# Attention, a dense layer and a top-2 expert layer in one kernel: three quarters of expert 0's converted weights are kept between its two parts

## The chip, the cores and the metric

One core of a Trainium2 chip runs the whole computation as one program. The metric is the device time of one execution in microseconds (us). The engines are TensorE (PE, with its weight loads shown apart as PEld), ScalarE (ACT), VectorE (DVE), GpSimd (POOL) and SyncE (SP). In this kernel SP issues the plain transfers between HBM and SBUF, and POOL issues the gathers and scatters that take their rows from a list.

## The reference

Three layers follow one another. All inputs are float32.

```
attention: q, k, v of 2 x 8 heads x 576 x 64
  scores = q k^T / 8; only the 32 largest of a row stay; softmax; times v
  -> x of 1152 tokens x 512
dense layer: h = x w_in (512 x 2048); g = max(h,0) + alpha min(h,0); x = g w_out (2048 x 512)
expert layer: 8 experts, each w1[e] (512 x 1024) and w2[e] (1024 x 512)
  logits = x w_gate + softplus(x w_noise) * noise; the best two experts of a token, softmax weights p
  out[token] = sum over its two experts of p * ( max(x w1[e], 0) w2[e] )
```

## The kernel before

**Precision.** Every float32 product is made of three matmuls on split operands. A weight tile is converted into a high part (a rounded copy, written by ACT) and a low part (raw minus high, written by DVE). The products are high times high, high times low and low times high.

**Order of the work.** The order of instructions on each engine is written out by a planner (class `Order`, line 136). Pieces of the kernel are generators that ask for an engine with a cost and a rank. The planner plays this through with its own clock and, whenever an engine is free in that play, emits the waiting step of lowest rank. The chip then runs each engine's list in that order, and each instruction waits for what it needs. Named counts such as `take("w2i", room=3)` and `give("w2i")` stand for buffers. When PE has nothing to do in the play, the planner may emit filler matmuls on a tile of ones (line 1728). It does so until the first block of expert 0's late part (line 1841).

**The dense layer** goes through the tokens in five groups of tiles. The last group (tiles 7 and 8) ends near 530 us. Behind it the gate runs for that group (`gate`, line 1051). It ranks the experts (a matmul into `pt`, line 1093, with the operand `g_ohb`), writes the slot lists with four scatters (line 1131, POOL), and expert 0's `oh` is made from `g_rm` (lines 1097 and 1239). When all groups have their slots, SP reads the lists back as `meta` (line 1187), and POOL gathers the tokens' rows by them (line 1323).

**The expert layer.** Each expert has 336 slots for tokens. Its weights are handled in four quarters `ch`, 256 of the 1,024 hidden columns each. A quarter has two halves: `half` 0 is a part of w1 (tile `w2i`) and `half` 1 a part of w2 (tile `w2o`). `weights2(e, ch, half, late)` (line 1271) takes one of five `raw2` buffers, loads 512 KB into it (for w1 of experts 0 and 1 in four transfers of 128 KB, line 1282; for w2 one transfer, line 1278), takes one of three `w2i` or `w2o` buffers, and converts with one ACT (line 1298) and one DVE instruction (line 1301) on 128x1024. The `raw2` buffer comes free after the DVE instruction.

**Expert 0 has two parts** (NE = 1). Slots are handed out in the order of the groups, and the kernel counts on the first four groups to fill its first 128 slots (a flag at the end tests that). So an early part can run while the last group's gate is being worked out: `early_block(0, ch)` (line 1417) for ch 0 to 3 does 12 matmuls of w1 (line 1438), two transposes (line 1452) and six matmuls of w2 (line 1472), and frees its `w2i` and `w2o` buffers behind each quarter. Then `x_part(0, d)` (line 1393) builds the operand for the other 208 slots in four steps, partly from `oh` (matmul at line 1408, ACT at line 1410, DVE at line 1412). The late part, `expert_block(0, fb)` (line 1482) for fb 0 to 7, does these 208 slots in blocks of half a quarter (12 matmuls at line 1507, the rest at line 1549). It goes through the quarters in the order 0, 1, 2, 3, and all four are loaded and converted a second time for it. An early quarter's buffers come free behind its early block. So the second conversions of quarters 0, 1 and 2 stand among the early blocks and the x_part steps, and those of quarter 3 behind block fb 1.

**Expert 1** follows. Its rows are gathered by `meta` and turned by PE (`x_part(1, d)`, line 1404). Its first weights take the buffers that expert 0's late part frees. Experts 1 to 7 use 336 slots in full.

Of the kernel before, what the change touches and what calls it, by code (L numbers as in the profile page):

```python
# [55 lines left out]
NE = 1  # L56
# [79 lines left out]
class Order:  # L136
# [107 lines left out]
    def give(self, what):  # L244
        self.held[what] -= 1
        self.given[what] = self.now
        self.at(self.now, 1, self.scan)

    def mark(self, *what):
        self.made.add(what)  # L250
        self.at(self.now, 1, self.scan)
# [12 lines left out]
def block_kernel(ctx: ExitStack, tc: tile.TileContext, q, k, v, w_in, w_out, alpha,  # L264
# [19 lines left out]
    order = Order()  # L284
# [986 lines left out]
    def weights2(e, ch, half, late=True):  # L1271
        yield need("b1")
        yield take("raw2", room=NRW)
        b1 = room["b1"]
        yield DMA, 1.5, 2.0
        raw = b1.tile([128, 1024], F32, name="raw2", bufs=NRW)
        if half:
            nc.sync.dma_start(raw.rearrange("p (c d) -> p c d", c=2),
                              w2[e][ch * 256:(ch + 1) * 256, :].rearrange("(c p) d -> p c d", p=128))
        elif e < NX:  # L1280
            for b in range(4):
                nc.sync.dma_start(raw[32 * b:32 * b + 32].rearrange("p (q f) -> p q f", q=4),
                                  w1[e][128 * b:128 * b + 128, ch * 256:(ch + 1) * 256].rearrange("(q p) f -> p q f", q=4))
        else:
            nc.sync.dma_start(raw.rearrange("p (c f) -> p c f", c=4),
                              w1[e][:, ch * 256:(ch + 1) * 256].rearrange("(c p) f -> p c f", p=128))
        tag = ("w2i", "w2o")[half]
        yield take(tag, room=3)
        wt = b1.tile([128, 2, 1024], R32, name=tag, bufs=3)
        W2[e, ch, half, late] = wt  # L1290
        turned = half and late and YT[0] <= e < YT[1]
        yield ACT, 0.95 + 0.1 * turned
        his, los, raws = [wt[:, 0]], [wt[:, 1]], [raw]
        if turned:
            his, los = ([in_order(wt[:, i, 512 * c:512 * c + 512]) for c in range(2)] for i in range(2))
            raws = [in_turns(raw[:, 512 * c:512 * c + 512]) for c in range(2)]
        for hi, x in zip(his, raws):
            nc.scalar.activation(hi, x, AF.Copy)  # L1298
        yield DVE, dve(1024) + 0.1 * turned
        for hi, lo, x in zip(his, los, raws):  # L1300
            V.tensor_sub(lo, x, split(hi))  # L1301
        yield FIN
        give("raw2")
        mark("w2", e, ch, half, late)

    def gather_x(e):
        yield need("b1")
# [109 lines left out]
    def early_block(e, ch):  # L1417

        yield need("w2", e, ch, 0, False)
        yield need("xe0", e)  # L1420
        for t in range(len(GROUPS[-1])):
            yield need("y1", len(GROUPS) - 1, 15)
        if (e, ch) != (0, 0):
            yield need("h0", *((e, ch - 1) if ch else (e - 1, 3)))
        else:
            yield take("yo", room=2)
            HN[0] = room["b1"].tile([128, CJ, DM], F32, name="yo", bufs=2).rearrange("p j d -> p (j d)")
        wh, wl = (W2[e, ch, 0, False][:, i].rearrange("p (c f) -> p c f", c=4) for i in range(2))
        xh, xl = (x[:, :, 0:CP] for x in XE[e])
        bank = yield take("h_ps", "s_ps")  # L1430
        steps = [(l, d, r) for d in range(4) for l, r in ((xh, wh), (xh, wl), (xl, wh))]
        for n, (l, d, r) in enumerate(steps):
            if n % 4 == 0:
                yield PE, 4 * 0.109
            if n == 0:
                h_ps = ps.tile([128, 2, 512] if bank == "s_ps" else [128, 512], F32, name=bank)
                h_ps = h_ps[:, 0, 0:256] if bank == "s_ps" else h_ps[:, 0:256]
            nc.tensor.matmul(h_ps, l[:, d, :], r[:, d, :], start=(n == 0), stop=(n == 11))
        mark("h0", e, ch)
        yield FIN  # L1440
        give("w2i")
        yield ACT, actp(256), 0, -EB
        hn = HN[0][:, 256 * ch:256 * ch + 256]
        nc.scalar.activation(hn, h_ps, AF.Relu)
        yield FIN
        give(bank)
        yield take("hh", room=3)
        bank = yield take("pt", "x_ps")
        yield PE, 0.22
        pt = ps.tile([128, 4, 128], F32, name=bank)  # L1450
        for i in range(2):
            nc.tensor.transpose(pt[:, i, :], hn[:, 128 * i:128 * i + 128], ident)
        yield ACT, actp(256), 0, -EB
        hh, hl = (room["b1"].tile([128, w], R32, name=n, bufs=3)[:, 0:256].rearrange("p (c t) -> p c t", c=2)
                  for n, w in (("hh", WIDTH), ("hl", CAP)))
        nc.scalar.activation(hh, pt[:, 0:2, :], AF.Copy)
        yield DVE, dve(256), 0, -EB
        V.tensor_sub(hl, pt[:, 0:2, :], split(hh))
        yield FIN
        give(bank)  # L1460
        if ch:
            yield need("y0", e, ch - 1)
        else:
            if not e:
                yield take("y")
            Y0[e] = ps.tile([128, DM], F32, name="y%d" % e)
        yield need("w2", e, ch, 1, False)
        bh, bl = (W2[e, ch, 1, False][:, i].rearrange("p (c d) -> p c d", c=2) for i in range(2))
        for i in range(2):
            yield PE, 0.648  # L1470
            for n, (l, r) in enumerate(((hh, bh), (hh, bl), (hl, bh))):
                nc.tensor.matmul(Y0[e], l[:, i, :], r[:, i, :], start=(ch == 0 and i == 0 and n == 0),
                                 stop=(ch == 3 and i == 1 and n == 2))
        mark("y0", e, ch)
        yield FIN
        give("hh")
        give("w2o")
        if (e, ch) == (NE - 1, 3):
            give("yo")
        mark("y0d", e, ch)  # L1480

    def expert_block(e, fb):

        ch, s = divmod(fb, 2)
        turned = YT[0] <= e < YT[1]
        yield need("w2", e, ch, 0, True)
        js = range(int(e < NE), CJ)
# [298 lines left out]
    for g, ts in enumerate(GROUPS):  # L1786
        t = max(t, ready[g])
        late = g == len(GROUPS) - 1
# [15 lines left out]
    FB = 3.7  # L1804
# [17 lines left out]
    for e in range(E):  # L1822
        te = t + e * TE
        if e < NX:
            ranks["xe", e] = te - 12.0
            order.add(te - 12.0, x_parts(e))
        if e >= NH:
            order.add(te - (XR if e >= NX else XN), gather_x(e))
        for ch in range(4):
            for half in range(2):  # L1830
                order.add(te + (2 * ch - 4 + half) * FB, weights2(e, ch, half))
        for fb in range(8):
            order.add(te + fb * FB, expert_block(e, fb))
        if e:
            order.add(te + 4 * FB, gather_partner(e))
        ranks["out", e] = te + TE
        order.add(te + TE, expert_out(e))
# [221 lines left out]
```

## Time and profile before

| what | value |
|---|---|
| time, median of 3 runs | 817.0 us (814.26 to 824.21) |
| the profiled execution: time | 811.02 us |
| its span, first to last instruction | 809.3 us |
| PE busy | 752.3 us (93%) |
| DVE busy | 606.2 us (75%) |
| ACT busy | 506.4 us (63%) |
| POOL busy | 358.1 us (44%) |
| data moved | 156.62 MB, mean 194 GB/s |

The profile is of one execution. Times are counted from the start of its span. An engine's busy time contains no register, branch or semaphore work; busy PE contains the filler matmuls too. A row of a timeline gives in brackets how long the engine sat idle before that instruction, and whose end released it by the profile's inference. The granted clock is 1.00 where PE has its full 2.4 GHz, and 0.50 where it has 1.2 GHz.

### The profile page before, as it was taken

The page shows a single profiled execution, that of the slowest core. Times are in us where ns is not written, and L with a number is a line of the kernel's source. Part 1 is how long each engine was busy: PE and PEld are TensorE (multiplying, and loading weights), DVE is VectorE, ACT ScalarE, POOL GpSimd, SP SyncE. Part 2 cuts the span into 40 slices and gives each one's busy share as a digit, 9 for nine tenths or more (in the row PEclk, how much of TensorE's full clock was granted, in tenths as well). Part 3 has the DMA queues.
Part 4 walks back from the last instruction along what each step waited for, and adds up shares of the span by engine and source line. Part 5 has one row for each costly group of instructions (what it writes and reads, how often), then busy time and mean ns, then how long its engine had stood idle before and what let it go on. Part 6 is the DMA issues. An engine that isn't in the chain of part 4 may idle for free. (4 is left out here: it accounts for less than half of the span.)

```text
span 809.3 us, 15510 instructions
## 1 busy us (share of the span) xinstructions
PE 752.3 (93%) x5238; PEld 685.8 (85%) x5238; DVE 606.2 (75%) x1713; ACT 506.4 (63%) x1081; POOL 358.1 (44%) x402
## 2 busy tenths in 40 slices
PE   8999878769999999999999999989899998999994
PEld 6888767668898998899988988878799997999983
DVE  6999999998988888898889545167567756667632
ACT  6878897897588778576747642264545544455331
POOL 3655665665575555454445434302422424131313
PEclk9999998688999999999999999999999999999998
DMA  9444689851446402465247559988889988986631
GB/s 277 138 157 122 196 284 321 291 177 64 134 148 193 156 28 94 150 229 181 104 132 234 183 181 304 347 218 198 239 247 242 264 212 245 254 255 180 203 103 59
DMA packets 99851, 156.62 MB, mean 194 GB/s; under 512 B 15902, under 2 KB 65582, under 8 KB 99764
## 3 DMA queue, kind: packets, MB, share of 16 engines
q1 hardware_dynamic: 94260, 145.04, 58.6%
q0 software_dynamic: 5504, 10.51, 4.5%
q8 instruction: 43, 0.70, 0.4%
q14 instruction: 44, 0.36, 0.1%
HBM read 126.76 MB, written 29.34 MB: 193 GB/s over the span
## 5 line engine op out<-in xcount | busy, mean ns | idle before, releaser
L672 POOL TENSOR_TENSOR low<-s_sb,low 128x576 f32<-128x576 f32 x72 | 102.5, 1425 | 81.6 <-ACT low L670 81.6
L948 PE MATMUL h_ps<-xh,wi 128*128 128x256 f32 (+1 forms) x576 | 123.9, 294 | 3.3 <-DVE gf L966 2.6
L948 PEld LDWEIGHTS h_ps<-xh,wi 128*128 128x128 f32 x576 | 98.0, 196 | 8.4 <-DVE gf L966 4.4
L633 DVE MAX8 tk<-rest 128x8 f32<-128x296 f32 x216 | 97.7, 459 | 1.1
L992 PE MATMUL y<-wo,gh 128*128 128x512 f32 x288 | 96.7, 417 | 1.3 <-ACT gh L976 1.3
L979 POOL TENSOR_TENSOR gl<-gf,gh 128x256 fp32r<-128x256 f32 (+1 forms) x80 | 56.6, 709 | 67.3 <-ACT gh L976 65.5
L948 PE MATMUL h_ps<-xl,wi 128*128 128x256 f32 (+1 forms) x288 | 83.4, 289 | 0.0
L717 PE MATMUL x_ps<-vb,pT 128*128 128x64 f32 (+1 forms) x640 | 79.7, 270 | 3.7 <-ACT pT L696 3.3
L717 PEld LDWEIGHTS x_ps<-vb,pT 128*128 128x128 f32 (+1 forms) x640 | 74.7, 187 | 9.9 <-ACT pT L696 6.6
L1298 ACT ACTIVATE w2o<-raw 128x512 fp32r<-128x512 f32 (+1 forms) x60 | 40.4, 711 | 57.2 <-PE x_ps L1542 31.6
L1301 DVE TENSOR_TENSOR w2o<-raw,w2o 128x512 fp32r<-128x512 f32 (+1 forms) x60 | 45.5, 790 | 35.6 <-ACT w2o L1298 28.8
L1507 PE MATMUL s_ps<-xeh,w2i 128*128 128x336 f32 (+1 forms) x256 | 64.9, 315 | 3.8 <-DVE hl L1523 3.8
L1542 PE MATMUL y<-hh,w2o 128*128 128x336 f32 (+1 forms) x288 | 66.9, 316 | 0.0
L636 DVE MATCH_REPLACE8 rest<-tk,rest 128x296 f32<-128x296 f32 x144 | 64.8, 451 | 0.0
L1507 PE MATMUL h_ps<-xeh,w2i 128*128 128x336 f32 (+1 forms) x256 | 63.3, 313 | 0.4 <-DVE hl L1523 0.4
L676 ACT ACTIVATE low<-low,bias 128x576 f32<-128x576 f32 x72 | 55.7, 774 | 12.3 <-POOL low L672 12.2
L582 PE MATMUL s_ps<-kp,qt 128*128 128x288 f32 (+2 forms) x336 | 60.9, 310 | 1.9 <-DVE rest L616 1.9
L598 ACT ACTIVATE s_sb<-s_ps 128x576 f32<-128x576 f32 x72 | 46.9, 651 | 22.9 <-PE s_ps L582 22.3
L992 PE MATMUL y<-wo,gl 128*128 128x512 f32 x144 | 58.6, 407 | 2.1 <-POOL gl L979 1.4
L670 ACT ACTIVATE low<-s_sb,bias 128x576 f32<-128x576 f32 x72 | 55.6, 774 | 7.7 <-POOL bias L641 7.6
L1323 POOL DMA_INDIRECT xg<-x,meta x21 | 25.7, 1225 | 72.2 <-DMA xl<-xg 28.9
L948 PEld LDWEIGHTS h_ps<-xl,wi 128*128 128x128 f32 x288 | 56.5, 196 | 0.7 <-issue 0.3
(315 smaller groups left out, 2069.4 us busy)
## 6 DMA issues: line engine op xcount, KB each, us to landing
raw<-in_moe_w_dram SPq DMA_DIRECT2D x60, 512.0 KB
wi<-wsc SPq DMA_DIRECT2D x48, 512.0 KB
wo<-wsc SPq DMA_DIRECT2D x48, 512.0 KB
raw<-in_moe_w_in_dram SPq DMA_DIRECT2D x16, 512.0 KB
raw<-in_moe_w_out_dram SPq DMA_DIRECT2D x16, 512.0 KB
wsc<-wi SPq DMA_DIRECT2D x16, 512.0 KB
wsc<-wo SPq DMA_DIRECT2D x16, 512.0 KB
raw<-in_moe_w_dram SPq DMA_DIRECT2D x48, 128.0 KB
```

The lines of the kernel that those rows point to most:

```text
L582: nc.tensor.matmul(s_ps[:, j, o:o + c1 - c0], l, r[:, c0:c1], start=(i == 0), stop=(i == len(steps) - 1 and (c < 4 or c1 != S)))
L633: V.max(tk[:, 8 * i:8 * i + 8], src)
L636: V.match_replace(rest, tk[:, 8 * i:8 * i + 8], src, -3.0e38)
L670: nc.scalar.activation(low, SC[ht], AF.Relu, bias=bi[:, 1:2], scale=-BIG)
L672: nc.gpsimd.tensor_sub(low, SC[ht], low)
L676: nc.scalar.activation(low, low, AF.Exp, bias=bi[:, 0:1], scale=SCALE, accum_out=SM[part][:, col:col + 1])
L717: nc.tensor.matmul(o, pT[:, i, cs], vb[b, hh // 2][:, s, i * 64:(i + 1) * 64], start=(first and hh == h and i == 0), stop=False)
L948: nc.tensor.matmul(h_ps, l[:, d, :], r[:, d, 0:gn], start=(n == 0), stop=(n == 11))
L979: nc.gpsimd.tensor_sub(gl, gf, split(gh))
L992: nc.tensor.matmul(Y1[g][t], l[:, t * 128:(t + 1) * 128], r, start=(i == 0 and n == 0), stop=(i == 15 and n == 2))
L1507: nc.tensor.matmul(h_ps, l[:, d, s * 128:(s + 1) * 128], r[:, d, :], start=(n == 0), stop=(n == 11))
L1542: nc.tensor.matmul(YP[e][b][:, 0:c], l[:, s, bs], r[:, 0:c], start=(fb == 0 and n == 0), stop=(fb == 7 and n == 2))
```

## The change

In the early part the buffers of quarters 1, 2 and 3 are no longer given back. Their tiles are entered a second time under the late part's key, and the late part's need is marked as met with the early one. The late part takes the quarters in the order 3, 2, 1, 0. Only quarter 0 is loaded and converted again. Its request stands at the rank that quarter 3 had, and it takes the buffer that comes free when the late part has used quarter 3. Experts 1 to 7 are asked for as before.

```
--- before.py
+++ after.py
@@ -1302,6 +1302,9 @@
         yield FIN
         give("raw2")
         mark("w2", e, ch, half, late)
+        if not late and ch:
+            W2[e, ch, half, True] = wt
+            mark("w2", e, ch, half, True)
 
     def gather_x(e):
         yield need("b1")
@@ -1438,7 +1441,8 @@
             nc.tensor.matmul(h_ps, l[:, d, :], r[:, d, :], start=(n == 0), stop=(n == 11))
         mark("h0", e, ch)
         yield FIN
-        give("w2i")
+        if not ch:
+            give("w2i")
         yield ACT, actp(256), 0, -EB
         hn = HN[0][:, 256 * ch:256 * ch + 256]
         nc.scalar.activation(hn, h_ps, AF.Relu)
@@ -1474,7 +1478,8 @@
         mark("y0", e, ch)
         yield FIN
         give("hh")
-        give("w2o")
+        if not ch:
+            give("w2o")
         if (e, ch) == (NE - 1, 3):
             give("yo")
         mark("y0d", e, ch)
@@ -1482,6 +1487,8 @@
     def expert_block(e, fb):
 
         ch, s = divmod(fb, 2)
+        if e < NE:
+            ch = 3 - ch
         turned = YT[0] <= e < YT[1]
         yield need("w2", e, ch, 0, True)
         js = range(int(e < NE), CJ)
@@ -1828,7 +1835,10 @@
             order.add(te - (XR if e >= NX else XN), gather_x(e))
         for ch in range(4):
             for half in range(2):
-                order.add(te + (2 * ch - 4 + half) * FB, weights2(e, ch, half))
+                if e >= NE:
+                    order.add(te + (2 * ch - 4 + half) * FB, weights2(e, ch, half))
+                elif ch == 3:
+                    order.add(te + (2 * ch - 4 + half) * FB, weights2(e, 0, half))
         for fb in range(8):
             order.add(te + fb * FB, expert_block(e, fb))
         if e:
```

## Rows read from the trace of the kernel before

**Rows 1.** Page, part 1: busy us over the span, share, instructions.
```profile
PE 752.3 (93%) x5238; PEld 685.8 (85%) x5238; DVE 606.2 (75%) x1713; ACT 506.4 (63%) x1081; POOL 358.1 (44%) x402
```

**Rows 2.** Stretches: length, busy PE, PEld, DVE, ACT, POOL, clock, DMA share, GB/s.
```profile
548.00:556.00 8.00, 7.24 (x51) 6.13 (x50) 7.86 (x19) 3.62 (x7) 4.75 (x4) 1.00 0.61 172
...
556.00:562.00 6.00, 6.00 (x44) 5.22 (x41) 2.40 (x5) 1.71 (x4) 0.00 (x0) 1.00 1.11 262
...
690.00:768.00 78.00, 78.00 (x509) 78.00 (x509) 52.50 (x87) 38.26 (x69) 22.10 (x18) 1.00 0.75 224
```

**Rows 3.** The same view, line 1301 alone: length, DVE, clock, DMA share, GB/s.
```profile
548.00:556.00 8.00, 5.86 (x5) 1.00 0.61 172
```

**Rows 4.** Instructions of lines 1298 and 1301: ns min/median/max, first and last start.
```profile
L1298 ACT ACTIVATE w2i<-raw x36: 1041/1052/1062, 477.0 to 771.2; 128x1024 fp32r<-128x1024 f32 x36
...
L1301 DVE TENSOR_TENSOR w2i<-raw,w2i x36: 1179/1225/1226, 478.1 to 772.3; 128x1024 fp32r<-128x1024 f32 x36
```

**Rows 5.** Timeline, PE, 545 to 557: start, us, line, operation [idle before, releaser].
```profile
545.11 0.17 PE L1093 MATMUL pt<-g_ohb,upper 128*128 128x8 bf16 x1 [1.33 <-DVE hl L1458]
...
550.92 0.82 PE L1728 MATMUL y<-ones 128*128 128x256 bf16 x6
...
552.23 0.67 PE L1406 MATMUL pt<-ident,xg 128*128 128x128 f32 x4 [0.49 <-DVE xel L1412]
...
554.90 1.47 PE L1728 MATMUL y<-ones 128*128 128x256 bf16 x12
...
556.13 0.34 PE L1507 MATMUL h_ps<-xeh,w2i 128*128 128x208 f32 x1
```

**Rows 6.** Timeline, ACT, 541 to 545.
```profile
541.96 1.06 ACT L1298 ACTIVATE w2i<-raw 128x1024 fp32r<-128x1024 f32 x1 [2.67 <-DMA raw<-in_moe_w_dram]
...
543.28 1.04 ACT L1298 ACTIVATE w2o<-raw 128x1024 fp32r<-128x1024 f32 x1
...
544.23 0.37 ACT L1456 ACTIVATE hh<-pt 128x256 fp32r<-128x256 f32 x1
```

**Rows 7.** Timeline, DVE, 544 to 551; five conversions stand from 549.54 to 556.
```profile
544.98 1.22 DVE L1301 TENSOR_TENSOR w2o<-raw,w2o 128x1024 fp32r<-128x1024 f32 x1
...
546.11 0.17 DVE L1097 SCALAR_TENSOR_TENSOR g_rm<-pt,g_ohb 128x16 f32<-128x16 f32 x1
...
549.46 0.17 DVE L1127 TENSOR_SCALAR mi<-g_pos 128x4 int32<-128x4 f32 x1
...
549.54 1.22 DVE L1301 TENSOR_TENSOR w2o<-raw,w2o 128x1024 fp32r<-128x1024 f32 x1
```

**Rows 8.** Timeline, POOL, 549 to 567: the four scatters and the first gather.
```profile
549.91 1.77 POOL L1131 DMA_INDIRECT slots<-mi,si  x1 [21.34 <-DVE mi L1127]
...
551.99 1.01 POOL L1131 DMA_INDIRECT slots<-mi,si  x1 [0.30 <-issue]
...
554.58 0.99 POOL L1131 DMA_INDIRECT slots<-mi,si  x1 [0.30 <-issue]
...
565.77 1.05 POOL L1323 DMA_INDIRECT xg<-x,meta  x1 [10.20 <-issue]
```

**Rows 9.** Timeline, SP's queue: the read of the slots.
```profile
560.53 0.38 SPq L1187 DMA_DIRECT2D meta<-slots  x1
```

**Rows 10.** Chain that ended last: start, us, what; two transfers' landings.
```profile
568.46 6.28 DMA xg<-x,meta
...
773.18 3.65 DMA ysc<-yo
```

**Rows 11.** Timeline, PE, 573 to 575: transposes of expert 1's rows.
```profile
573.99 0.33 PE L1404 MATMUL pt<-ident,xg 128*128 128x128 f32 x1 [1.74 <-issue]
...
574.78 0.29 PE L1404 MATMUL pt<-ident,xg 80*128 80x80 f32 x1 [0.47 <-DMA xg<-x,meta]
```

**Rows 12.** Timeline, PE, at 681; then the stretch behind it, as rows 2.
```profile
681.75 0.42 PE L1507 MATMUL s_ps<-xeh,w2i 128*128 128x336 f32 x1 [3.78 <-DVE hl L1523]
...
681.70:685.20 3.50, 3.45 (x13) 3.46 (x14) 3.50 (x7) 2.48 (x6) 0.00 (x0) 0.57 0.60 186
```

More of the change, by code (lines that the diff above doesn't have):

```diff
@@ L1304, in weights2 @@
         mark("w2", e, ch, half, late)
+        if not late and ch:
+            W2[e, ch, half, True] = wt
+            mark("w2", e, ch, half, True)
     def gather_x(e):
@@ L1440, in early_block @@
         yield FIN
-        give("w2i")
+        if not ch:
+            give("w2i")
         yield ACT, actp(256), 0, -EB
@@ L1476, in early_block @@
         give("hh")
-        give("w2o")
+        if not ch:
+            give("w2o")
         if (e, ch) == (NE - 1, 3):
@@ L1484, in expert_block @@
         ch, s = divmod(fb, 2)
+        if e < NE:
+            ch = 3 - ch
         turned = YT[0] <= e < YT[1]
@@ L1830, in block_kernel @@
             for half in range(2):
-                order.add(te + (2 * ch - 4 + half) * FB, weights2(e, ch, half))
+                if e >= NE:
+                    order.add(te + (2 * ch - 4 + half) * FB, weights2(e, ch, half))
+                elif ch == 3:
+                    order.add(te + (2 * ch - 4 + half) * FB, weights2(e, 0, half))
         for fb in range(8):
```

## Prediction

> **What bounds the kernel now.** I read the page first, then the busy times by stretch, then the timelines of PE, ACT, DVE, POOL and SP around the change, and last the chain that ended last. The page shows PE busy for 752.3 of 809.3 us [rows 1]. The stretches say where that holds. From 690 to 768, in the middle of the expert layer, PE is busy for 78.00 of 78.00 us, and what is done on another engine there is hidden [rows 2]. From 548 to 556, between expert 0's early and late part, DVE is the full engine: 7.86 of 8.00 us, of which the conversions of line 1301 are 5.86 us in five instructions [rows 2, 3]. PE looks busy there too, but part of it is filler on `ones` [rows 5]. So a gain has to come out of the few places before expert 1 where PE waits or fills.
>
> I find four such places. The gate's matmul at 545.11 came after 1.33 us of idle time, released by DVE's `hl` [rows 5]. From 550.92 to 552.23 there are six fillers and a wait of 0.49 us for `xel`, together 1.31 us [rows 5]. From 554.90 to 556.13 there are twelve fillers before the late part's first matmul, 1.23 us [rows 5]. And the transposes of expert 1's rows wait 1.74 and 0.47 us for the gather [rows 11]. Beside PE runs a second path: the gate's last DVE step at 549.46, four scatters, SP's read of the slots at 560.53, POOL's gather from 565.77, its landing 6.28 us behind 568.46, at 574.74 [rows 7 to 10]. Both paths meet at the transposes, and there the gather is the later one.
>
> **What is removed.** Six of the eight second conversions go, with their loads. On ACT that is 6 x 1.05 = 6.3 us, on DVE 6 x 1.22 = 7.3 us [rows 4]. On SP it is 3 x 4 + 3 x 1 = 15 transfers of 6 x 512 KB = 3 MB. In time the places that empty are the early ones, those of quarters 0, 1 and 2. The pair that stays stands where quarter 3's pair stood, behind block fb 1. No matmul goes.
>
> **PE's own path.** The wait of 1.33 us: ACT's `hh` at 544.23, which feeds that `hl`, stood behind a second conversion (541.96, which had itself waited 2.67 us for its load) and an early one (543.28) [rows 6]. The first goes, so ACT can be 1.06 us or more ahead. The price lies between 0 and 1.33 us, and I take 1.33, since the queue loses 1.06 us of work and 2.67 us of waiting. The 1.31 us: the `xel` steps stand between conversions of 1.22 us on DVE, all five from 549.54 on are second ones, and all five go [rows 3, 7]. Between 0 and 1.31, I take 1.31. The 1.23 us of fillers cover the same queue ahead of the last `xel`, and go too. PE reaches the transposes 1.33 + 1.31 + 1.23 = 3.87 us earlier.
>
> **The gather's path.** The gate's chain on DVE starts with `g_rm` at 546.11, right behind a conversion of 544.98 that ends at 546.20 (starts and ends overlap by the pipeline) [rows 7]. Its matmul is at 545.11 [rows 5]. The matmul moves by 1.33 us. The wait behind the conversion, 546.11 - 545.11 = 1.00 us less the matmul, is gained as well if that early conversion moves ahead. So between 1.33 and 2.3 us; I take 1.8. The last scatter ends at 554.58 + 0.99 = 555.57, and SP can read at 560.53, so landing takes 4.96 us, and the read 5.24 us until the first gather at 565.77 [rows 8, 9]. Both lie in a stretch with a DMA share of 1.11 [rows 2], which is weight loads. With five `raw2` buffers, the loads that are next after the early part (expert 0's quarter 0, expert 1's quarter 0, half of its quarter 1) all fit at once, and are done before the scatters; the next one has to wait for a conversion behind fb 1. For an emptier path the nearest row is a store that landed in 3.65 us [rows 10]. So the landing gains 0 to 1.3 us and the read 0 to 1.6 us. I take 0.7 for each, the middle, since one row of another kind is not much. The first scatter took 1.77 us and a later one 1.01 us [rows 8]. That gives 0 to 0.8 us, and I take 0, since the later ones also ran beside conversions. The gather itself stays amid weight loads: 0. The sum is 1.8 + 0.7 + 0.7 = 3.2 us, between 1.3 and 6.0.
>
> On that first scatter the Trainium skill has a rule. SBUF — State Buffer, section "SBUF: two separate sides", says that GpSimd cannot write its descriptors while VectorE holds the port pair that they share. By that, all 0.8 us would come back and the gather's path would gain 4.0 us. The trace agrees only in part: the scatters at 551.99 and 554.58 started among the same conversions and took 1.01 and 0.99 us [rows 8].
>
> **The sum.** If the transposes keep their place in PE's list, PE gets what the gather's path gains, 3.2 us, and waits 2.21 + 3.87 - 3.2 = 2.9 us there. If the planner puts them further behind (it emits them when its own play has the gather landed, and in its play too PE moves further than the gather), the late part's remaining blocks fill that wait, and at most 3.87 + 2.21 = 6.1 us come back. I take 4.0, nearer the lower end because the play is not the chip. From there PE is full [rows 2], so the gain stays until the end. The span becomes 809.3 - 4.0 = 805.3, and the profiled execution 811.0 - 4.0 = 807.0. The median of the runs shown is 6.0 above that execution, so on its scale the time is 817.0 - 4.0 = 813.0.
>
> **Costed at nothing.** Quarter 0's second conversion has to be done between fb 1, which frees the buffer, and fb 6. Four blocks cover it, as they covered quarter 3's. Without that cover it would cost 1.05 + 1.22 = 2.3 us. Expert 1's first conversions wait for the buffer that fb 3 frees, before and after. POOL's queue holds none of the moved steps. Quarter 0's ACT instruction now waits for the readers of quarter 3, as quarter 3's did for those of quarter 0. Behind it on ACT stand the relus of fb 2 and later, and PE's next blocks wait for those, before and after.
>
> **The rivals.** *Off the path, nothing comes back.* No PE work is removed, and the gather ends the stretch; if scatters and reads land as slowly as before, and `g_rm` keeps its place behind other DVE work, only 0 to 1.3 us are gained: 816.5. For it speaks that the wait at the transposes is the last to end [rows 11]; against it, that four things on the gather's path become lighter at once. The Trainium skill's Perfetto Trace Analysis, section "Identifying the Most-Contended Engine", says to improve the most contended engine first, which is PE by the page and is not touched here. The trace agrees for the stretch from 690, not for the one from 548.
>
> *The read of the slots gets stuck on SP (slower).* SP works in order. Loads that wait for a `raw2` buffer now wait for conversions behind fb 1, later than before relative to the gate. Each load listed ahead of the read holds it until one more pair of 1.05 + 1.22 = 2.27 us is through. Three of them put the read at 552.3 (the late part's start, 556.13 - 3.87) + 6.8 = 559.1 at the earliest, plus the blocks' own matmuls between. It decides once the read starts later than 560.53, so with three or more. One or two further pairs make the gather 2.3 to 4.5 us later than before, and PE, which comes 3.87 us earlier, waits over 6 us for it. At 681 a wait of 3.78 us was followed by 3.5 us at a granted clock of 0.57, between its levels of 1.2 and 2.4 GHz [rows 12], which cost 3.5 x 0.43 = 1.5 us. Together 3.8 to 6.0 us slower, 4.9 in the middle: 821.9. Against it: the planner gives the read the lowest rank of all, and one or two loads ahead cost little.
>
> *The plan changes elsewhere.* The order behind the change is worked out anew. The wait of 3.78 us and its slow clock at 681 [rows 12], 5.3 us, may go: 813.0 - 5.3 = 807.7. Or one more of that size appears: 818.3. The rows don't say which.
>
> **How the numbers follow.** Likeliest, as summed: 0.60, at 813.0, with a range of its own from 808 to 818 (gain 1.3 to 6.1, and the runs before lay from 2.7 below to 7.2 above their median). Nothing comes back: 0.17, 816.5. The read gets stuck: 0.08, 821.9. A wait elsewhere goes 0.08, 807.7, or comes 0.07, 818.3. The range from 804 to 821 leaves out most of the stuck read and the far ends of the runs' scatter, under 0.2. A measurement of this kernel can tell about 2% from no change, that is below 800.7 or above 833.3. Waits and fillers before expert 1 sum to 6.1 us, so the first needs 10 us from elsewhere: 0.03. The second needs two mishaps of the sizes above: 0.03. Within 2%: 0.94.
>
> **What would show it.** In the profile after: six conversions fewer on ACT and on DVE, so 33 for `w2i` instead of 36 [rows 4], and 15 transfers fewer on SP; no second conversion on DVE between the gate's chain and the last `xel`; few or no fillers before the late part; the late part's first matmul near 552.3; the read of the slots near 557 to 558; the transposes' wait at 2 to 3 us or filled. The prediction is wrong if the late part starts earlier and the gather does not, if a load stands ahead of the read on SP, or if PE waits somewhere behind 582 where it did not before.

## The result, and the profile after

The changed kernel took 802.9 us (median of five runs, 801.13 to 804.16). The kernel before took 816.0 beside it (five runs, 813.12 to 824.21). The ratio on record, estimated from fast executions alone, is 0.9879, with an interval from 0.9836 to 0.9921; the two medians by themselves would give 0.9839. That is 1.2% faster: within 2% as forecast, but more than twice the 4.0 us that were summed. On the scale of 817.0, which the prediction used, the ratio gives 807.1 us, inside its range of 804 to 821. The median as it stands lies 1.1 us below that range. The profiled execution took 802.91 us with a span of 801.1 us, where before had 811.02 and 809.3.

Page of after, part 1: busy us, share of the span, instructions (beside [rows 1]).

```profile
PE 752.0 (94%) x5230; PEld 687.7 (86%) x5230; DVE 600.1 (75%) x1707; ACT 501.7 (63%) x1075; POOL 361.1 (45%) x402
```

Line 1301 of after: ns min/median/max, first and last start, forms (beside [rows 4]).

```profile
L1301 DVE TENSOR_TENSOR w2i<-raw,w2i x33: 1183/1225/1227, 479.3 to 764.4; 128x1024 fp32r<-128x1024 f32 x33
```

The work that was to go is gone: 33 conversions of `w2i` in place of 36, six instructions fewer on ACT and six on DVE, and 153.48 MB moved in place of 156.62. PE's busy time is the same within 0.3 us, while the span is 8.2 us shorter. What went is waiting.

Stretches of after, with the columns of [rows 2].

```profile
548.00:556.00 8.00, 7.74 (x52) 7.02 (x50) 4.85 (x29) 1.68 (x5) 3.03 (x3) 1.00 0.28 67
556.00:562.00 6.00, 6.00 (x43) 5.15 (x41) 2.35 (x4) 1.98 (x4) 1.38 (x2) 1.00 0.13 11
690.00:768.00 78.00, 78.00 (x500) 76.97 (x499) 52.48 (x86) 38.93 (x69) 20.42 (x15) 1.00 0.72 208
```

From 548 to 556 DVE is busy for 4.85 us in place of 7.86. The larger change is the last but one column: from 556 to 562 the DMA share is 0.13 in place of 1.11.

Timeline of PE in after: start, us, line, operation, idle time before it and its releaser (beside [rows 5]).

```profile
547.41 0.82 PE L1735 MATMUL h_ps<-ones 128*128 128x256 bf16 x6
548.49 0.17 PE L1093 MATMUL pt<-g_ohb,upper 128*128 128x8 bf16 x1 [0.26 <-DVE hl L1462]
...
556.07 0.60 PE L1735 MATMUL y<-ones 128*128 128x256 bf16 x4
556.42 0.34 PE L1514 MATMUL h_ps<-xeh,w2i 128*128 128x208 f32 x1
```

Timelines of POOL and of SP in after (beside [rows 8, 9]): the first and the last scatter and the first gather, then the loads and the read of the slots.

```profile
552.27 1.05 POOL L1131 DMA_INDIRECT slots<-mi,si  x1 [21.25 <-DVE mi L1127]
...
556.22 0.98 POOL L1131 DMA_INDIRECT slots<-mi,si  x1 [0.30 <-issue]
561.60 1.25 POOL L1326 DMA_INDIRECT xg<-x,meta  x1 [4.40 <-issue]
```

```profile
548.13 1.74 SPq L1282 DMA_DIRECT2D raw<-in_moe_w_dram  x4
558.34 0.38 SPq L1187 DMA_DIRECT2D meta<-slots  x1
561.95 0.38 SPq L1278 DMA_DIRECT2D raw<-in_moe_w_dram  x1
```

SP issues no load between 549.9 and 561.95, while the scatters land and the slots are read. In the kernel before five half quarters, 2.5 MB, were still issued between 550.82 and 558.42, and the read at 560.53 came behind them. What held it last was the landing of the scatters, though, and not SP's own work: SP still waited 1.8 us for them. Waits of SP in before from 540 to 575, the row of the read: line, what it waited for, us, times, longest.

```profile
SPq L1187 <- DMA slots<-mi,si: 1.8, 1, 1.8
```

The absolute times of the two executions can't be set side by side as they are, because the dense layer ends at a different time in each. The early part's first matmul started at 530.69 in before and at 533.38 in after, though every engine's list is the same up to there. The table counts from that matmul, E. X is expert 1's first matmul, and "end" is PE's last one. "Landing" is from the end of the last scatter to the read of the slots, "read" from there to the first gather, and "wait" is PE's idle time at expert 1's transposes. The profiles of the experiments below are in it too.

| kernel (profiled execution) | E | gate's matmul - E | late part - E | landing | read | first gather - E | wait | X - E | end - X | time |
|---|---|---|---|---|---|---|---|---|---|---|
| before | 530.69 | 14.42 | 25.44 | 4.96 | 5.24 | 35.08 | 2.21 | 51.28 | 216.87 | 811.02 |
| before, second profile | 531.47 | 16.85 | 27.89 | 4.28 | 4.74 | 36.33 | 2.59 | 55.63 | 211.86 | 811.14 |
| before, third profile | 532.36 | 16.40 | 27.42 | 4.60 | 5.16 | 36.63 | 1.95 | 54.52 | 216.75 | 815.80 |
| after | 533.38 | 15.11 | 23.04 | 1.14 | 3.26 | 28.22 | 0 | 46.14 | 211.20 | 802.91 |
| after, second profile | 533.83 | 14.32 | 22.26 | 1.16 | 3.15 | 27.35 | 0 | 45.36 | 213.16 | 804.53 |
| order 1, 2, 3, 0 | 533.75 | 15.32 | 23.26 | 1.15 | 3.11 | 28.30 | 0 | 46.35 | 211.85 | 804.14 |
| loads stay | 527.84 | 14.28 | 22.23 | 6.65 | 5.90 | 35.54 | 6.61 | 55.17 | 211.12 | 806.32 |
| conversions stay | 532.45 | 13.72 | 24.74 | 3.08 | 4.30 | 31.56 | 0 | 48.90 | 219.09 | 812.63 |
| before, one load sooner | 531.96 | 16.78 | 27.81 | 4.09 | 5.09 | 36.43 | 2.05 | 53.43 | 213.09 | 812.20 |
| before, step 3.8 | 533.49 | 15.65 | 26.68 | 6.98 | 6.75 | 39.85 | 8.10 | 61.34 | 210.06 | 817.41 |
| after, step 3.8 | 532.88 | 14.58 | 22.51 | 1.15 | 3.09 | 27.53 | 0 | 45.61 | 212.13 | 802.81 |
| before, loads behind the read | 533.22 | 15.78 | 26.79 | 1.51 | 3.05 | 30.80 | 0 | 50.95 | 217.94 | 814.30 |
| after, hl first | 529.91 | 12.83 | 21.65 | 1.15 | 3.16 | 26.90 | 0 | 45.61 | 211.53 | 800.20 |

Where PE waits at the transposes, it can lose more than the wait. The stretch behind that wait in "loads stay" (6.61 us of waiting) and in before's second profile (2.59 us), with the columns of [rows 2]:

```profile
574.50:580.00 5.50, 5.47 (x27) 5.43 (x28) 1.20 (x3) 1.41 (x4) 0.00 (x0) 0.55 0.54 173
```

```profile
578.30:585.00 6.70, 6.68 (x40) 6.34 (x41) 3.51 (x8) 3.65 (x9) 2.25 (x3) 0.75 0.81 219
```

PE is busy there, but at a granted clock of 0.55 and 0.75. By these rows that costs an estimated 5.5 x 0.45 = 2.5 us and 6.7 x 0.25 = 1.7 us more. In the first profile of before (2.21 us of waiting) and in both of after (none) the granted clock stays at 1.00 in this place; in before's third profile (1.95 us) it is 0.68 from 579 to 583. This is a good part of why X - E differs by 4 us between the first two profiles of one kernel; the other part is the late part's start, 2.45 us later in the second.

### The profile page after: what moved, and what is told of

Read it like the earlier page. It is cut to its first block, busy times and chain, and to the rows that moved or that the text cites. A ratio compares the mean times of both kernels' runs of the same rounds, so it can differ in the third digit from the quotient of the medians.

```text
span 801.1 us, 15451 instructions
## 1 busy us (share of the span) xinstructions
PE 752.0 (94%) x5230; PEld 687.7 (86%) x5230; DVE 600.1 (75%) x1707; ACT 501.7 (63%) x1075; POOL 361.1 (45%) x402
## 2 busy tenths in 40 slices
DMA packets 97307, 153.48 MB, mean 192 GB/s; under 512 B 15662, under 2 KB 63806, under 8 KB 97220
## 4 chain that ended last, share of the span: by engine, by line
PE 71%; ACT 9%; issue 6%; DVE 5%; DMA 4%; POOL 3%; SPq 0%; another core or an unknown queue 0%; POOLq 0%; ACTq 0%; DVEq 0%
PE h_ps L948 10%; PE y L992 9%; PE y L1549 8%; PE x_ps L717 7%; PE h_ps L1514 6%; PE s_ps L1514 6%; PE s_ps L582 4%; PE y L1735 3%; PE x_ps L1549 3%; PE pt L693 2%; PE pt L423 2%; DMA raw<-in_moe_w_dram 1%; PE y L1556 1%; ACT low L676 1%; PE y L423 1%
## 5 line engine op out<-in xcount | busy, mean ns | idle before, releaser
L1298 ACT ACTIVATE w2o<-raw 128x512 fp32r<-128x512 f32 (+1 forms) x57 | 37.2, 693 | 57.4 <-PE x_ps L1549 37.1
L1301 DVE TENSOR_TENSOR w2o<-raw,w2o 128x512 fp32r<-128x512 f32 (+1 forms) x57 | 41.9, 769 | 33.6 <-ACT w2o L1298 30.5
L1514 PE MATMUL s_ps<-xeh,w2i 128*128 128x336 f32 (+1 forms) x256 | 62.8, 310 | 0.0
L992 PEld LDWEIGHTS y<-wo,gh 128*128 128x128 f32 x288 | 49.5, 193 | 8.1 <-ACT gh L976 1.8
```

What stands on the lines that cost most here:

```text
L992: nc.tensor.matmul(Y1[g][t], l[:, t * 128:(t + 1) * 128], r, start=(i == 0 and n == 0), stop=(i == 15 and n == 2))
L1514: nc.tensor.matmul(h_ps, l[:, d, s * 128:(s + 1) * 128], r[:, d, :], start=(n == 0), stop=(n == 11))
```

## The experiments

Two theories were set against each other. A: the gain before expert 1 is on the gather's path, and comes from the loads that no longer stand ahead of the scatters and of the read. B: it comes from the conversions that DVE and ACT no longer do. A third question was what lies behind expert 1, where the wait at 681 [rows 12] was gone.

### The changed kernel again, and the quarters in natural order

> The changed kernel unaltered, so that the next three runs stand beside it on one chip, and to see which of its differences from the kernel before come again. If the gain is a property of the two orders: about 803 us, 1.2% under the kernel before; the late part's first matmul 23 us behind the early part's first; the first gather 28 us behind it; PE full (30.0 of 30 us) between 660 and 690, so no wait of 3.8 us near 681. If a part of it was chance of one execution: the early part starts some 2.7 us sooner again, and the time falls towards 800, or a wait of some 4 to 5 us is back in the stretch from 660 to 690 and the time is near 808.

Measured: 804.2 us (801.2 to 805.6), ratio 0.9885 (0.984 to 0.9931). The distances come again within 0.9 us, and PE is busy for 29.87 of 30 us from 660 to 690.

The second run only takes the quarters in another order:

```
-            ch = 3 - ch
+            ch = (ch + 1) % 4
```

> The changed kernel with the late part's quarters in the order 1, 2, 3, 0 in place of 3, 2, 1, 0. Theory that the gain comes from the three kept quarters alone, in whatever order: within 2 us of the changed kernel, late part's start and first gather at the same distance behind the early part (23 and 28 us). Rival, that the turned order itself matters, since quarter 3 is converted last and is the one that the late part wants first: the late part would then start up to 1 us sooner with quarter 1 first, as that was converted long before. Since the planner works out everything behind it anew, a wait elsewhere (some 5 us near 681 in the kernel before) may come back: then 808.

Measured: 803.7 us (801.68 to 805.26), ratio 0.9884 (0.984 to 0.9927). The turned order as such makes no difference that can be measured. The gain needs the three kept quarters and not their order; quarter 0 comes last in both.

### The loads stay, the conversions go

```
+                else:
+                    order.add(te + (2 * ch - 4 + half) * FB, load_again(e, ch, half))
```

`load_again` takes a `raw2` buffer, issues the transfers of `weights2` and gives the buffer back when the early part has used the quarter behind it. Nothing reads what it loads.

> The changed kernel, but quarters 0 to 2 are still loaded a second time at the ranks that the second conversions had (15 transfers, 3 MB, not converted and not used). Theory A, that the gather's path gained from the transfers that are gone: the scatters' landing and the read are slow again (4 to 5 us and 5 us in place of 1.1 and 3.3), the first gather comes 32 to 35 us behind the early part's first matmul in place of 28, expert 1 starts 2 to 5 us later, time 805 to 808. Theory B, that it gained from the DVE and ACT instructions that are gone: the first gather stays at 28 us, the time stays within 1 us of the changed kernel. Both: the late part's first matmul stays at 23 us behind the early part's first.

Measured: 809.8 us (806.32 to 814.72), ratio 0.997 (0.9937 to 1.0002). Of the gain some 5.6 us are lost again, a little more than theory A gave (805 to 808). Timelines of PE and POOL:

```profile
549.72 0.60 PE L1751 MATMUL y<-ones 128*128 128x256 bf16 x4
...
571.88 0.45 PE L1423 MATMUL pt<-ident,xg 128*128 128x128 f32 x1 [4.88 <-DMA xg<-x,meta]
573.48 0.48 PE L1423 MATMUL pt<-ident,xg 128*128 128x128 f32 x1 [1.16 <-DMA xg<-x,meta]
574.53 0.40 PE L1423 MATMUL pt<-ident,xg 80*128 80x80 f32 x1 [0.57 <-DMA xg<-x,meta]
```

```profile
545.91 1.05 POOL L1131 DMA_INDIRECT slots<-mi,si  x1 [19.32 <-DVE mi L1127]
```

Its PE path is that of after: 22.23 us to the late part. Its gather's path is that of before: 35.54 us to the first gather, with a landing of 6.65 us. The result is a wait of 6.61 us, about what the prediction had priced for its slower rival, but with another cause. With the slow clock behind it (0.55, above) expert 1 starts 9.4 us later behind E than in after's two profiles, where 2 to 5 had been expected. Timeline of SP:

```profile
551.43 4.17 SPq L1282 DMA_DIRECT2D raw<-in_moe_w_dram  x4
557.48 0.38 SPq L1187 DMA_DIRECT2D meta<-slots  x1
```

Loads stand ahead of the read, but none of them waits for a buffer. To issue four took 4.17 us, where it takes 1.74 in after, and the read had to wait for the scatters even then. The transfers themselves were slow: while it issued these four, SP waited for earlier loads. This is theory A for the gather's path.

### The conversions stay, the loads go

```
+                else:
+                    order.add(te + (2 * ch - 4 + half) * FB, convert_again(e, ch, half))
```

`convert_again` copies the kept tile's high part with ACT into a `raw2` buffer and subtracts on DVE, both 128x1024. The result is not used.

> The changed kernel without the second loads, but with six idle pairs of ACT copy and DVE subtraction of 128x1024 from the kept tiles, at the ranks that the second conversions had (their result is not used). Theory B, that the gain before expert 1 comes from DVE: six fillers and the wait for xel are back, so the late part's first matmul comes 25 us behind the early part's first in place of 23, the first scatter takes 1.7 us again in place of 1.05, and the time is 805 to 807. Theory A, that transfers set the gather's path: the read of the slots and the first gather stay near 28 us behind the early part's first matmul, and the time is within 1.5 us of the changed kernel, with PE waiting less at the gather.

Measured: 811.0 us (807.38 to 817.44), ratio 0.9983 (0.9945 to 1.002). Timelines of PE, POOL and SP:

```profile
551.97 0.82 PE L1749 MATMUL y<-ones 128*128 128x256 bf16 x6
...
555.96 1.47 PE L1749 MATMUL y<-ones 128*128 128x256 bf16 x12
...
614.67 0.65 PE L1528 MATMUL h_ps<-xeh,w2i 128*128 128x336 f32 x1 [2.53 <-ACT xeh L1382]
```

```profile
550.97 1.77 POOL L1131 DMA_INDIRECT slots<-mi,si  x1 [19.77 <-DVE mi L1127]
```

```profile
555.81 0.39 SPq L1278 DMA_DIRECT2D raw<-in_moe_w_dram  x1
556.95 1.74 SPq L1282 DMA_DIRECT2D raw<-in_moe_w_dram  x4
559.71 0.38 SPq L1187 DMA_DIRECT2D meta<-slots  x1
```

Here it is the other way round. The fillers are back in both places, six and twelve, and the first scatter takes 1.77 us. The late part starts 24.74 us behind E, 2.1 us later than the 22.65 of after's two profiles. The landing lies between, at 3.08 us, because the idle pairs hold the `raw2` buffers and push two of expert 1's loads to 555.81, onto the scatters. The 3.2 us lost at X (48.90 against a mean of 45.75) fit theory B's 805 to 807. The time doesn't: it lost 6.8 us against after. The rest arises behind X, with the wait of 2.53 us above and a granted clock of 0.83 from 608 to 618. ACT's `xeh` stood there behind a step that waited 3.52 us for a gathered tile `wi`.

The two halves differ in their plans too. Behind X the lists of PE, ACT and DVE in the run with the loads are, instruction for instruction, those of after. In the run with the conversions they are nearly those of before: the last 1,056 of PE's 1,327 matmuls come in the same order. So the time behind X (211.12 against 219.09 us) was measured under two different plans, and whether the idle pairs as such cost anything there is open. The two halves don't add up either: at X they cost 9.4 and 3.2 us, together more than the 8.1 us that the whole change gained there.

### The loads of the other experts wait for the read

The kernel before, with all second loads and conversions; only the loads of experts 1 to 7 start later (in `weights2`, ahead of the `take`):

```
+        if e:
+            yield need("meta")
```

> The kernel before, with all its second loads and conversions, but the loads of experts 1 to 7 wait until the slots have been read. Theory A, that the gather's path is slowed by the loads that stand ahead of the read: only expert 0's own loads are left there, issued up to 553, so the landing of the scatters falls from 4 to 5 us to 1 to 2 and the read from 5 to 3.3; the first gather comes 30 to 32 us behind the early part's first matmul in place of 35 to 36, and with expert 1's weights still in time the kernel is 2 to 5 us faster than before. Theory B, that it is the conversions on DVE and ACT: landing and read stay above 4 us. A loss would mean that expert 1's first weights come too late: a wait for w2i at its first matmul.

Measured: 813.0 us (806.57 to 819.4), ratio 0.9971 (0.9939 to 1.0003). Timelines of SP and PE:

```profile
556.55 0.38 SPq L1280 DMA_DIRECT2D raw<-in_moe_w_dram  x1
560.97 0.38 SPq L1187 DMA_DIRECT2D meta<-slots  x1
561.46 1.94 SPq L1284 DMA_DIRECT2D raw<-in_moe_w_dram  x4
```

```profile
606.33 0.65 PE L1544 MATMUL y<-hl,w2o 128*128 128x336 f32 x1 [3.21 <-DVE hl L1525]
...
686.27 0.42 PE L1509 MATMUL s_ps<-xeh,w2i 128*128 128x336 f32 x1 [2.40 <-DVE hl L1525]
```

All conversions are there, and the landing takes 1.51 us and the read 3.05, as in after. So it is the transfers that set both, not the engines. The wait at the transposes is gone, and X is 2.9 us nearer to E than the mean of before's three profiles (50.95 against 53.81). The kernel as a whole gains nothing that can be measured, where theory A had 2 to 5 us: two waits behind X, 3.21 and 2.40 us, take it back. The transfers are only put off here, not removed. Whether that is why PE waits later is not shown.

### Is the wait at 681 the plan's or the execution's?

> The kernel before unaltered, for a second profile of it. If the wait of 3.8 us at 681 and the slower clock behind it are a property of its order of work: they are there again, with PE busy about 26 of 30 us from 660 to 690, and the early part, the late part and the first gather are at the same distances (25.4 and 35.1 us behind the early part's first matmul). If they were chance of one execution: the wait is under 1 us. The early part's first matmul, 530.7 in the first profile, shows by how much the layers ahead of the change vary (533.4 in the changed kernel).

> The kernel before, a third profile. Theory that its time varies with how late the second loads land before expert 1: expert 1's first matmul anywhere from 581 to 588, ACT's second conversion at 542 to 546 waiting 2 to 5 us for its load, the slots' landing at 4 to 5 us, and whatever this execution is slower or faster than 811 shows in that matmul's time or in a wait near 681. Rival, that it varies in the layers ahead of 530: the early part's first matmul moves by as much as the end does.

Measured: 811.1 and 815.8 us. The same wait was 1.12 us in the second profile and 2.24 us in the third, against 3.78 in the first. The place is the plan's, the size is the execution's. In the third profile another wait, 2.11 us at 623, stands beside it. The two profiles show something else, which the first didn't have. Timelines of ACT and PE in the second:

```profile
545.17 1.06 ACT L1298 ACTIVATE w2i<-raw 128x1024 fp32r<-128x1024 f32 x1 [4.39 <-DMA raw<-in_moe_w_dram]
546.13 0.36 ACT L1444 ACTIVATE yo<-s_ps 128x256 f32<-128x256 f32 x1
```

```profile
546.55 0.44 PE L1452 MATMUL x_ps<-ident,yo 128*128 128x128 f32 x2 [1.76 <-ACT yo L1444]
...
683.16 0.42 PE L1507 MATMUL s_ps<-xeh,w2i 128*128 128x336 f32 x1 [1.12 <-issue]
```

ACT's second conversion waited 4.39 us for its load (4.25 in the third profile, 2.67 in the first [rows 6]). The relu `yo` stood behind it, and PE's transposes waited 1.76 us (1.65 in the third) for that. In the first profile the load came just early enough for PE not to wait there.

> The kernel before, with the rank of one load alone (expert 4, w2 of quarter 2) 3.7 us lower. All is as before up to expert 3; behind it the planner's order is another. Theory that the wait at 681 comes from that load standing late in SP's list behind small copies: the load is issued some microseconds sooner, ACT's conversion doesn't hold up the relu, no wait over 1 us from 660 to 690, and the time falls by 4 to 5 us, to about 808 on the scale of a kernel before at 812.5. Rival, that the transfers as a whole are too much there: the wait moves to the next load or stays, time within 2 us of the kernel before.

The edit, in the kernel before:

```
+                sooner = 1.0 * FB if (e, ch, half) == (4, 2, 1) else 0.0
+                order.add(te + (2 * ch - 4 + half) * FB - sooner, weights2(e, ch, half))
```

Measured: 814.1 us (808.21 to 820.74), ratio 1.0005 (0.9957 to 1.0053). The wait there is 0.67 us, and the kernel isn't faster. The theory that this one load was worth 4 to 5 us falls; the other two profiles of before pay only 1.12 and 2.24 us there.

### Another plan for both

```
-    FB = 3.7
+    FB = 3.8
```

> The kernel before, with the planner's step between two blocks' ranks 3.8 in place of 3.7, which gives the expert layer another order without changing the work. Theory that the difference of 5.3 us behind 600 is a draw of the plan, and that before drew a bad one: within the range from 5 us faster to 3 us slower than before, with the gather's path as before (first gather 33 to 36 us behind the early part's first matmul). Rival, that the second loads and conversions lead to such waits in any plan: it has waits of 3 us or more behind 600 as well, and is within 2 us of before.

> The changed kernel with the same other step of 3.8. The gain before expert 1 (about 5 us) should stay in any plan: the late part's first matmul 23 us and the first gather 28 us behind the early part's first, and 4 to 6 us faster than the kernel before with that step. If the gain behind 600 belongs to the change too: 7 to 9 us faster than that kernel. If it is a draw of the plan: anything from 2 us slower to 10 us faster.

Measured: before with this step 813.9 us (807.54 to 817.41), ratio 1.0 (0.9962 to 1.0038); after with it 804.4 us (800.78 to 811.39), ratio 0.9922 (0.9883 to 0.9961). Between the two are 9.5 us. So the gain comes in both plans and not in one lucky plan alone. With this step the kernel before has no wait over 0.3 us behind X at all, but 8.10 us at the transposes and a landing of 6.98 us. Its costs have moved; their sum hasn't. From X to the end it took 210.06 us, 2.1 us less than after with this step (212.13). So in this pair the whole gain lies before X, 61.34 against 45.61 us behind E.

### The term that failed on PE's path

The changed kernel, with an added mark behind `hl` in `early_block`:

```
         V.tensor_sub(hl, pt[:, 0:2, :], split(hh))
         yield FIN
         give(bank)
+        mark("hl", e, ch)
...
+        if half and not late and ch == 3:
+            yield need("hl", e, 2)
         yield ACT, 0.95 + 0.1 * turned
```

> The changed kernel, with the early conversion of w2's quarter 3 held back until the hl of early block 2 is done. The gate's matmul waits there for hl (1.08 us of filler and idle time), and hl stands on DVE behind that conversion. Theory: the gate's matmul comes 1.0 us sooner after the early part's first matmul (14.1 in place of 15.1 us), and the scatters and the first gather 1 to 1.3 us sooner; but the fillers go to another place ahead of the late part, whose first matmul gains 0 to 0.5 us, and since PE didn't wait for the gather any more, the time stays within 1 us of 803 to 804. Rival, that the gate's chain still sets PE's path: 1 to 1.3 us faster.

Measured: 801.9 us (800.2 to 804.2), ratio 0.9849 (0.9799 to 0.99). Timelines of PE, POOL and DVE:

```profile
542.74 0.17 PE L1093 MATMUL pt<-g_ohb,upper 128*128 128x8 bf16 x1
...
544.34 0.83 PE L1738 MATMUL h_ps<-ones 128*128 128x256 bf16 x6
```

```profile
546.53 2.10 POOL L1131 DMA_INDIRECT slots<-mi,si  x1 [17.89 <-DVE mi L1127]
```

```profile
546.49 1.21 DVE L1303 TENSOR_TENSOR w2o<-raw,w2o 128x1024 fp32r<-128x1024 f32 x1
```

The gate's matmul no longer waits. It comes 12.83 us behind E in place of 15.11 and 14.32, a gain of more than the 1 us expected. Six fillers (0.83 us) moved behind it, as expected. The late part starts some 1 us sooner (21.65), and X stays where it was (45.61). The lowest median of all is this kernel's, but its ratio lies inside the interval of the changed kernel's, so it isn't shown to be better.

## Why the prediction was right, and where it wasn't

**The sum against the runs.** The means of the profiles give the balance. X - E went from 53.81 (three profiles) to 45.75 (two): 8.1 us. The stretch from X to the end went from 215.2 to 212.2: 3.0 us. E itself came 2.1 us later, in a part that the change doesn't touch. Together that is 8.9 us, as between the means of the profiled times (812.7 and 803.7). The prediction had 4.0 us for the first and nothing for the second. The first is clear of the profiles' scatter (51.28 to 55.63 before, 45.36 and 46.14 after). The second is not: before's three profiles took 211.86 to 216.87 us from X to the end, after's two 211.20 and 213.16. Against the one execution that the prediction read, X - E fell by 5.1 us, inside the 3.2 to 6.1 that its sum allowed.

**Right.** What goes from each queue; that PE's busy time doesn't change; that the gain arises at the four places and no load gets stuck ahead of the read; that the first loads all fit into the five `raw2` buffers and are through before the scatters; that the planner may put the transposes further behind, so that PE doesn't wait for the gather at all (the wait is 0 in every profile of after); that quarter 0's conversion is covered.

**PE's own path: 3.87 us forecast, 2.40 against the first profile.** Of the three terms the middle one, 1.31 us, came in full. Of the twelve fillers ahead of the late part four stay, 0.35 us, so 0.9 of 1.23 came. The gate's matmul kept 1.08 of its 1.33 us. The step that failed is "the queue loses 1.06 us of work and 2.67 us of waiting". That was ACT's queue. On DVE the early conversion of quarter 3, which stays, now stands directly ahead of the `hl` that the matmul waits for. Timeline of DVE in after:

```profile
546.87 1.23 DVE L1301 TENSOR_TENSOR w2o<-raw,w2o 128x1024 fp32r<-128x1024 f32 x1 [0.48 <-ACT w2o L1298]
548.02 0.42 DVE L1462 TENSOR_TENSOR hl<-pt,hh 128x256 fp32r<-128x256 f32 x1
```

The run with `hl` first shows it: the wait goes when that conversion stands behind. Against the mean of before's profiles the path gained 4.27 us (26.92 to 22.65), near the sum, but by another mixture. The transposes' wait of 1.7 us for `yo` is in it, which the first profile didn't show.

**The gather's path: 3.2 us forecast, 6.9 against the first profile, outside its bounds of 1.3 to 6.0.** The terms: 0.3 for the gate's chain (1.8 taken), 0.7 for the first scatter (0 taken), 3.8 for the landing (0.7 taken, 1.3 at most) and 2.0 for the read (0.7 taken, 1.6 at most). The step that failed is the row for an emptier path. A store at the kernel's end that landed in 3.65 us [rows 10] was taken as the floor, and 1.14 us is what these scatters take in a stretch with a DMA share of 0.13. The rows from 556 to 562 with their DMA share of 1.11 [rows 2] had shown that the landing ran under a full DMA. The argument had itself found that those loads would be gone by then; it should have let the bound reach far lower. That the time came out near the range all the same is in part luck: the transposes were planned further behind, so PE no longer waited for the gather, and the size of that path no longer set the time.

The Trainium skill gives a direction for this. DMA: Bandwidth & Descriptors, section "Latency and other measured facts", says that HBM access takes much longer under high load than on average, and that a lighter load makes the fixed cost of a transfer smaller. The runs agree: 1.1 to 1.5 us with few transfers ahead, 4 to 7 us with many. That the time is lost at HBM, and not in the queues, is not shown.

**The first scatter, and the rule weighed there.** It took 1.77 us in all three profiles of before and 1.05 in both of after. The two halves tell the cause: 1.05 with the loads and without the conversions, 1.77 with the conversions and without the loads. In the run with `hl` first, a conversion starts at 546.49 and the scatter of 546.53 beside it takes 2.10 us. In all eight profiles in which a conversion was running when the first scatter started, the scatter ended 0.92 or 0.93 us behind the end of that conversion, whether it had started 0.04 us into it or 0.37 us. So the 0 that was taken was wrong by 0.7 us. The rule of the Trainium skill (SBUF — State Buffer, "SBUF: two separate sides"), by which GpSimd can't write its descriptors while VectorE holds the shared ports, fits this scatter.

The prediction held the later scatters against the rule, since they started among the same conversions and took 1.01 and 0.99 us. Timeline of DVE in before:

```profile
552.09 1.21 DVE L1301 TENSOR_TENSOR w2o<-raw,w2o 128x1024 fp32r<-128x1024 f32 x1
...
553.51 1.21 DVE L1301 TENSOR_TENSOR w2i<-raw,w2i 128x1024 fp32r<-128x1024 f32 x1
```

The scatter of 551.99 started 0.10 us ahead of a conversion, that of 553.30 as it ended, and that of 554.58 0.14 us before the next one's end [rows 8]. None had more than that to wait for, so they don't speak against the rule. That the ports are the reason is not shown: the conversion of 552.09, which started while a scatter ran, took its usual 1.21 us.

**Behind expert 1.** That "the gain stays until the end" held, and in these profiles there was more. The wait at 681 was named as a rival with a chance of 0.08. It went, in every profile of after. Stretch from 660 to 690 of before and of after: length, PE busy, granted clock, DMA share, GB/s.

```profile
660.00:690.00 30.00, 26.22 (x159) 0.94 0.88 239
```

```profile
660.00:690.00 30.00, 30.00 (x196) 1.00 0.96 262
```

It isn't worth the 5.3 us that the first profile suggests, since other executions of before lose 1.1 or 2.2 us there. From X to the end the means differ by 3.0 us, which the scatter of the profiles covers, and with the other step the difference has the other sign. The removed transfers are not what takes the wait away. In the run where the loads stay and the plan behind X is that of after, PE is as full from 660 to 690 (length, PE busy, granted clock, DMA share, GB/s), and X to the end takes 211.12 us.

```profile
660.00:690.00 30.00, 30.00 (x197) 1.00 0.94 265
```

So the other order behind X is the likelier reason; what in it helps wasn't settled. The prediction put the new order behind X at nothing in its sum and had it only as a rival. A small new wait came with that order, 1.09 us for `fb` near 610. "PE waits somewhere behind 582 where it did not before" was one of the prediction's own signs of being wrong, and this one came true, at a small price.

**The base and the range.** The prediction set its sum against one execution and put the difference to the runs' median, 6.0 us, on top unexplained. A good part of it was that 817.0 was high: the 57 further runs of the kernel before, beside the experiments, had medians of 812.5, 814.2 and 813.7. The place before expert 1 was cheap in that execution (X - E 51.28 against 55.63 and 54.52), but this alone doesn't explain the difference, since the second profile paid 4.4 us more there, 5.0 us less behind X, and took 811.14. The median fell below the range because its cases were treated as exclusive: the top of the first case, 6.1 us back, and the wait at 681 going, 5.3 us. Both came, each in part. That they have one root is not shown. The upper end of the likeliest case, 818, doesn't follow from the scatter that it names (817.0 - 1.3 + 7.2 = 822.9).

**The rival "nothing comes back"** is gone. PE is the busiest engine and none of the computation's matmuls went, and still expert 1 started 8.1 us nearer to E.

## What to carry to other kernels

Price a removed transfer by what stands behind it, not by its bytes: the loads issued among four small scatters and the read that waits for them made landing and read 5.8 us longer, which no engine's busy time shows. Where a wait ends on a DMA, one profile shows one draw of it: the same wait was 3.78, 1.12 and 2.24 us in three profiles of one kernel. A wait of PE is priced with the granted clock behind it, not by its length alone. And two cases that don't exclude each other can both come, so the range must hold their sum.

## What the runs showed of the hardware

From the end of small scatters to the read that waits for them it took 1.1 us where few transfers were in flight, and from that read of 60 KB to the gather behind it 3.1 to 3.3 us. Beside weight loads at a DMA share of about 1 it was 4 to 7 and 4.7 to 6.8 us. The first of four scatters on POOL took 1.05 us alone; where a DVE conversion of 1.2 us was running at its start, it took 1.76 to 2.10 us and ended 0.92 or 0.93 us behind that conversion. Scatters that started ahead of a conversion or in the last 0.2 us of one took 1.0 us. After waits of 2.59 and 6.61 us at the transposes PE's granted clock was 0.75 and 0.55 for 6.7 and 5.5 us, between its levels of 1.2 and 2.4 GHz; after 2.21 us in another profile it was 1.00. The start of the early part, up to which every engine's list is the same in all kernels here, lay between 527.8 and 533.8 us in thirteen profiles.
